# Attention's second 1024 tokens loaded in six transfers by token groups, and half of the state model's first input behind their transposes

## Chip, cores and metric

The kernel runs on one core of one Trainium2 chip. The metric is the device time of one execution in microseconds (us); less is better. A core has a matrix engine (TensorE, "PE" in the profile), a vector engine (VectorE, "DVE"), an activation engine (ScalarE, "ACT"), GpSimd ("POOL") and a queue engine (SyncE, "SP") that here does nothing but issue transfers. Sixteen DMA engines move the data. An engine executes its own instructions in order; between engines, semaphores make one wait for another.

## What is computed

Two independent models read two inputs of 2048 tokens x 448 features and give the two halves of one output of 2048 x 896. The first is an attention in which a token looks at eight tokens, at distances 0, 2, ..., 14 behind it, with 16 heads of 28. The second is a state-space model with 448 complex states.

```python
# first half: A (D = 448, H = 16, Dh = 28, W = 8, dil = 2)
qkv = x @ wqkv                                  # q, k, v
idx = pos[:, None] - arange(W) * dil            # masked where negative
logits = einsum("bhsd,bhswd->bhsw", q, k[idx]) * Dh ** -0.5
o = einsum("bhsw,bhswd->bhsd", softmax(logits), v[idx])
a = o @ wo
# second half: B
Lam_bar = exp(dt * Lam); B_bar = ((Lam_bar - 1) / Lam) * Bmat
h_t = Lam_bar * h_{t-1} + B_bar @ x_t           # complex, 2048 steps
y = 2 * real(C @ h) + x * Dskip
return concatenate([a, b], axis=-1)
```

## The kernel before

All work is cut into small operations, and a list written out by hand (`ORDER`, lines 32 to 61) gives the order in which they are put on the engines. A name of the list is an operation with its arguments; `@` gives the PSUM banks, and the last sign the engine that empties them.

**Attention.** Tokens are handled as two units of 1024, called u = 0 and u = 1. For both, the input has to stand transposed in the tile `xT` (features on the partitions). Its chunks are [128 features, 512 tokens]; chunk 3 holds the last 64 features of both 512-token halves. For u = 0, TensorE transposes the input. For u = 1 the DMA engines do: line 167 loads the tokens 1024 to 2047 into the second half of the buffer `xbuf` in three transfers, one for each range of columns, each for all four groups t of 128 rows (group t stands for the 128 tokens from 1024 + 128 t and the 128 tokens from 1536 + 128 t). Line 182 issues four DMA transposes, one for each t, from `xbuf` to `xT[:, 1]`. The operations `QK1..` (query and key projections, all four groups) and `V_4..`, `V_5..` (value projections; `V_4..` takes the groups 0 and 1, `V_5..` the groups 2 and 3) read the result. The first of them in `ORDER` are `V_411` and `V_410`; behind these comes `QK100`.

**The state model's input** is loaded by `x_load` (lines 174 to 177) into `xnB`, in four column blocks cb of 128 chunks: `x_load(0)` brings cb 0 and 1 in six transfers, `x_load(1)` cb 2 and 3. It is transposed by DMA later (`xt`, line 746, in the order cb 2, 0, 1, 3) into `xbuf`, when attention no longer needs that buffer. The weight `Bn` (line 187) is loaded between, and transposed by `BD` (line 722). The first operations that read all four transposed blocks are `BU200` and `BU100`, which begin the state model on TensorE.

**The queue engine.** Nearly all transfers are issued by SP, in program order: weights and attention's input; the three of line 167; the six of `x_load(0)`; the four transposes of line 182; four of `Bn`; the six of `x_load(1)`; four of `Cr` (the operation `LC`, lines 288 and 289); then `TD0` (line 451), the DMA transpose of the first unit's logits, which ScalarE writes in `lt` (line 442); then `xt` and `BD`. An issue that must wait holds back all that is behind it. The transfers take turns on eight semaphores, so an issue also waits until the transfer eight places before it has landed.

Of the kernel before, what the change touches and what calls it, by code (L numbers as in the profile page):

```python
# [14 lines left out]
S, D, H, DH, W = 2048, 448, 16, 28, 8  # L15
# [48 lines left out]
def kernel(  # L64
# [21 lines left out]
    SP = nc.sync  # L86
# [37 lines left out]
    xA_r = A_x[0].rearrange("(t p) d -> p t d", p=128)  # L124
# [38 lines left out]
        w_half(s, 0, D, 2 * D)  # L163

    xA1 = xbuf[:, 8 * D:].rearrange("p (t n) -> p t n", n=2 * D)
    for d0, d1, b, c in ((0, D, 8, 0), (D, 512, 12, 384), (512, 896, 12, 0)):
        SP.dma_start(xA1[:, :, d0:d1], xA_r[:, b:b + 4, c:c + d1 - d0])


    xnB = keep.tile([128, 4, T, D], BF16, tag="xnB")  # L170
    xP = xnB.rearrange("p c j d -> p c (j d)").rearrange("p c (a n) -> p c a n", a=2)
    xB_r = B_x[0].rearrange("(q p h a b) d -> h p q a b d", q=2, p=128, h=2, a=2)

    def x_load(hh):
        for d0, d1, b, c in ((0, D, 0, 0), (D, 512, 1, 384), (512, 896, 1, 0)):
            for q in range(2):
                SP.dma_start(xP[:, 2 * hh + q, :, d0:d1], xB_r[hh, :, q, :, b, c:c + d1 - d0])

    x_load(0)

    for t in range(4):
        SP.dma_start(xT[:, 1, :, 128 * t:128 * t + 128], xA1[:, t], transpose=True)

    Bn = s2.tile([128, G, 512], BF16, tag="Bn")
    for d0, d1, c in ((0, D, 0), (D, 512, 384)):
        for ri, b in enumerate((B_B_re, B_B_im)):
            SP.dma_start(Bn[64 * ri:64 * ri + 64, :, d0:d1], b[:, c:D].rearrange("(g p) d -> p g d", p=64))
    x_load(1)
    dsk = const.tile([128, 2 * D], BF16, tag="dsk")

    ident = const.tile([128, 128], BF16, tag="ident")
# [843 lines left out]
```

## Time and profile before

| | us |
|---|---|
| three runs | 125.88, 123.89, 125.00 |
| median | 125.0 |
| the profiled execution | 123.66 |
| its span, from the first to the last instruction | 121.9 |
| TensorE busy in the span | 117.4 |
| VectorE / ScalarE busy | 110.5 / 103.9 |
| granted TensorE clock | 1.00 of full speed |

The profile is of one execution. Its times count from the first instruction; 1.8 us of the 123.66 lie outside the span. "L258" is line 258 of the kernel; a line of a helper (258 is the matmul inside `part`, 114 the eviction) stands for many operations. `out<-in` names the tiles. "SPq" is an issue on SP's queue: its length is the time that SP needs to issue, not that of the transfer. "Time to landing" is from the start of an issue until the data is in place. A list of waits says which engine was held up by what. The chain of waits goes back from the last instruction, at each step to what released it.

### The profile page before, as it was taken

The numbers are of one execution on the slowest core, as the hardware profiler recorded it, in microseconds if no ns is written. First come the engines' busy times: TensorE is split into PE (matmuls) and PEld (weight loads), VectorE is DVE, ScalarE is ACT, GpSimd is POOL, SyncE is SP. The second block draws the span as 40 slices with busy tenths as digits, with TensorE's granted clock in tenths as the row PEclk, the third lists the DMA queues.
The fourth block names the chain that finished last, engine by engine and source line by source line (L and its number), as shares of the span: only waits on it lengthen the run. The fifth ranks groups of instructions, "written<-read, shape, count | busy, mean of one in ns | idle before, by whom it ended". The sixth has DMA issues, their size and how long they took to land.

```text
span 121.9 us, 2888 instructions
## 1 busy us (share of the span) xinstructions
PE 117.4 (96%) x1071; PEld 59.3 (49%) x1071; DVE 110.5 (91%) x198; ACT 103.9 (85%) x200; POOL 22.6 (19%) x49
## 2 busy tenths in 40 slices
PE   6989999999999999999999999999999999999990
PEld 6765434432434443363345544645665555555560
DVE  4378999999999999999999999999999999998561
ACT  0799999989999999999999999999999999980000
POOL 6823600000000000004999910000000000000000
PEclk9999999999999999999999999999999999999999
DMA  3999999999899999789869999999642504436642
GB/s 92 259 277 245 320 213 206 190 190 269 271 200 207 214 213 142 182 171 369 258 104 147 140 316 260 129 126 132 163 98 47 155 0 147 134 117 199 199 151 75
DMA packets 56661, 22.34 MB, mean 183 GB/s; under 512 B 42343, under 2 KB 56103, under 8 KB 56647
## 3 DMA queue, kind: packets, MB, share of 16 engines
q1 hardware_dynamic: 56440, 22.08, 83.6%
q8 instruction: 8, 0.13, 0.4%
q10 hardware_dynamic: 207, 0.07, 0.3%
q14 instruction: 6, 0.05, 0.1%
HBM read 9.86 MB, written 6.37 MB: 133 GB/s over the span
## 4 chain that ended last, share of the span: by engine, by line
PE 92%; DMA 4%; ACTq 1%; DVE 0%; issue 0%
PE ps L258 40%; PE ps L916 16%; PE ps L585 10%; PE ps L429 5%; PE ps L773 4%; PE ps L572 4%; DMA wzz<-in_A_wqkv_dram 4%; PE ps L373 3%; PE ps L846 1%; PE ps L941 1%; PE ps L374 1%; PE ps L433 1%; ACTq L150 1%; PE ps L499 1%; PE ps L385 1%; PE ps L785 1%
## 5 line engine op out<-in xcount | busy, mean ns | idle before, releaser
L417 DVE TENSOR_TENSOR pr<-qf,kf 128x2048 bf16<-128x2048 bf16 x24 | 27.7, 1219 | 0.2 <-ACT qf L114 0.2
L258 PE MATMUL ps<-xbuf,BT 128*128 128x512 bf16 (+1 forms) x112 | 24.1, 380 | 0.0
L916 PE MATMUL ps<-Cw,Z 128*128 128x448 bf16 x105 | 20.8, 352 | 0.0
L258 PE MATMUL ps<-xT,wq 128*128 128x512 bf16 (+1 forms) x72 | 15.8, 380 | 0.0
L916 PEld LDWEIGHTS <-Z 128*128 128x128 bf16 x105 | 10.3, 98 | 9.5
L258 PEld LDWEIGHTS <-BT 128*128 128x128 bf16 (+1 forms) x112 | 9.0, 97 | 11.7 <-issue 3.2
L585 PE MATMUL ps<-wo,oT 128*128 128x448 bf16 x64 | 13.4, 353 | 0.0
L258 PE MATMUL ps<-wq,xT 128*128 128x448 bf16 (+1 forms) x64 | 12.0, 353 | 0.0
L114 ACT CAST Z<-ps 128x512 bf16<-128x512 f32 (+1 forms) x23 | 11.4, 537 | 0.3 <-PE ps L258 0.2
L992 POOL MEMSET PT<- 128x4320 f32 x3 | 11.0, 3703 | 0.0
L258 PEld LDWEIGHTS <-wq 128*128 128x128 bf16 (+1 forms) x72 | 6.0, 97 | 8.7 <-issue 2.5
L734 ACT ACTIVATE ctmp<-Cw,c2t 64x448 f32<-64x448 bf16 x14 | 9.3, 666 | 0.2
L585 PEld LDWEIGHTS <-oT 128*128 128x128 bf16 x64 | 6.2, 98 | 5.7
L114 ACT CAST oT<-ps 128x512 bf16<-128x512 f32 x15 | 8.2, 626 | 0.0
L114 ACT CAST v_s<-ps 128x448 bf16<-128x448 f32 x16 | 8.2, 536 | 0.0
L258 PEld LDWEIGHTS <-xT 128*128 128x128 bf16 (+1 forms) x64 | 5.2, 97 | 6.3 <-issue 1.8
L968 POOL MEMSET Z<- 128x14 bf16 x1 | 0.1, 112 | 42.3 <-ACT ctmp L734 42.3
L114 ACT CAST qf<-ps 128x512 bf16<-128x512 f32 x12 | 7.0, 590 | 0.5 <-PE ps L258 0.5
L773 PE MATMUL ps<-Z,R 128*128 128x512 bf16 x21 | 7.3, 381 | 0.0
L114 ACT CAST kf<-ps 128x512 bf16<-128x512 f32 x12 | 7.0, 591 | 0.0
L114 ACT CAST ya<-ps 128x448 bf16<-128x448 f32 (+1 forms) x12 | 6.1, 552 | 0.2 <-PE ps L585 0.2
L926 DVE TENSOR_TENSOR xbuf<-ps,xnB 128x384 bf16<-128x384 f32 x8 | 4.4, 549 | 2.0 <-PE ps L916 2.0
(175 smaller groups left out, 228.2 us busy)
## 6 DMA issues: line engine op xcount, KB each, us to landing
PT<-pd SPq DMA_DIRECT2D x16, 156.0 KB, 4.3
out_dram<-ya SPq DMA_DIRECT2D x16, 112.0 KB, 1.7
out_dram<-xbuf SPq DMA_DIRECT2D x15, 112.0 KB, 1.8
pd<-Ak SPq DMA_DIRECT2D x2, 640.0 KB, 3.6
xbuf<-in_A_x_dram SPq DMA_DIRECT2D x2, 448.0 KB, 5.0
xnB<-in_B_x_dram SPq DMA_DIRECT2D x4, 224.0 KB
xnB<-in_B_x_dram SPq DMA_DIRECT2D x4, 192.0 KB, 4.2
pd<-oT SPq DMA_DIRECT2D x1, 640.0 KB, 5.1
```

The costliest lines, as they stand in the source:

```text
L114: (ACT.copy if e == "A" else V.tensor_copy)(o, i)
L258: PE.matmul(o, l, r, start=(first and i == 0), stop=(not first and i == len(pairs) - 1 and not more[s]))
L373: PE.matmul(p[:], wqk(m, slice(0, 128), kt), xT[:, 0, 4 * s + kt], start=(kt == 0), stop=False)
L417: V.tensor_tensor(t[:], q.unsqueeze(1).to_broadcast((128, 4, 512)), k4, ALU.mult)
L429: PE.matmul(acc[s][32 * i:32 * i + 32], E[:, f, ws, :], t[:, i, :], start=(f == 0 and ws == 0), stop=False)
L572: PE.matmul(p[32 * hh:32 * hh + 32, 128 * bl:128 * bl + n], v_s[:, t, 4 * hg + hh, :], PT[:, t % NS, (4 * hg + hh) // HS, (4 * hg + hh) % ...
L585: PE.matmul(p[:, 0:D], late["oT"][:, b // 4, hg, par, 128 * (b % 4):128 * (b % 4) + 128], late["wo"][:, hg, :], start=(hg == 0), stop=(hg ...
L734: ACT.activation(t[a:a + 64, 0:D], Cw[b:b + 64, g, :], ACTF.Copy, scale=c2t[a:a + 64, g:g + 1])
L773: PE.matmul(pp["z", g, j][:], rot(g, 0), late["Z"][:, g, j - 1, :], start=False, stop=True)
L916: PE.matmul(p[:, 0:D], z, Cw[:, g, :], start=(g == 0), stop=(g == G - 1))
L926: V.tensor_tensor(yo[:, 0:384], p[:, 0:384], xP[:, ct, j // 2, 512:896], ALU.add)
L992: POOL.memset(late["PT"][:, 4 * i:4 * i + 4].rearrange("p t g n -> p (t g n)").bitcast(F32), 0.0)
```

## The change

The load of attention's second unit is cut by token groups: three transfers for the groups 0 and 1, then three for 2 and 3, each half as large. `x_load` takes a list of blocks and brings one block after the other. The transfers of cb 1, three of the six of `x_load(0)`, are issued behind the four transposes. `x_load(1)` brings the same six transfers as before, with cb 2 whole before cb 3.

```diff
-    for d0, d1, b, c in ((0, D, 8, 0), (D, 512, 12, 384), (512, 896, 12, 0)):
-        SP.dma_start(xA1[:, :, d0:d1], xA_r[:, b:b + 4, c:c + d1 - d0])
+    for t in (0, 2):
+        for d0, d1, b, c in ((0, D, 8 + t, 0), (D, 512, 12 + t, 384), (512, 896, 12 + t, 0)):
+            SP.dma_start(xA1[:, t:t + 2, d0:d1], xA_r[:, b:b + 2, c:c + d1 - d0])
...
-    def x_load(hh):
-        for d0, d1, b, c in ((0, D, 0, 0), (D, 512, 1, 384), (512, 896, 1, 0)):
-            for q in range(2):
+    def x_load(hh, *qs):
+        for q in qs:
+            for d0, d1, b, c in ((0, D, 0, 0), (D, 512, 1, 384), (512, 896, 1, 0)):
                 SP.dma_start(xP[:, 2 * hh + q, :, d0:d1], xB_r[hh, :, q, :, b, c:c + d1 - d0])
 
-    x_load(0)
+    x_load(0, 0)
 
     for t in range(4):
         SP.dma_start(xT[:, 1, :, 128 * t:128 * t + 128], xA1[:, t], transpose=True)
+    x_load(0, 1)
...
-    x_load(1)
+    x_load(1, 0, 1)
```

## The prediction

> **What bounds the kernel now.** I read the page first, then the list of waits for TensorE, then the chain of waits in order of time.
>
> ```profile
> span 121.9 us, 2888 instructions
> PE 117.4 (96%) x1071; PEld 59.3 (49%) x1071; DVE 110.5 (91%) x198; ACT 103.9 (85%) x200; POOL 22.6 (19%) x49
> PE 92%; DMA 4%; ACTq 1%; DVE 0%; issue 0%
> ```
>
> TensorE is busy for 117.4 of 121.9 us, and 92% of the chain that ended last lies on it. The profiled execution took 123.66 us, so 1.8 us lie outside the span. The three runs took 123.89, 125.00 and 125.88: the profiled one is 1.34 below their median.
>
> ```profile
> PE ps L276 <- DVE wz L120: 1.1, 1, 1.1
> PE ps L386 <- DMA wzz<-in_A_wqkv_dram: 0.4, 1, 0.4
> ...
> 6.56 0.05 issue
> 6.61 0.28 PE ps L386
> ...
> 15.70 4.77 PE ps L258 x26
> 20.47 1.41 PE ps L429 x24
> 21.88 6.28 PE ps L258 x32
> ...
> 117.60 1.36 PE ps L941 x14
> 118.98 0.39 DVE xbuf L951
> ```
>
> The first two rows are all the waits that TensorE had, and both are over by 6.61 us, before the first changed instruction. From then on the chain is TensorE, piece against piece (15.70 + 4.77 = 20.47; 20.47 + 1.41 = 21.88), until the last matmul at 118.96. So in this execution the transposed second unit never held TensorE up. That is the first result: there is nothing here for an earlier arrival to win. A change of the loads can cost, where it makes TensorE wait, and can win only in executions that ran less smoothly than the profiled one.
>
> The timeline of TensorE has the two consumers that matter, and that of SP the issues around the change:
>
> ```profile
> 21.82 1.61 PE L258 MATMUL ps<-wq,xT 64*128 64x448 bf16 x8
> 23.26 2.75 PE L258 MATMUL ps<-xT,wq 128*128 128x512 bf16 x12
> ...
> 48.29 3.52 PE L258 MATMUL ps<-xbuf,BT 128*128 128x512 bf16 x18
> ```
>
> ```profile
> 9.09 1.69 SPq L167 DMA_DIRECT2D xbuf<-in_A_x_dram  x3
> 10.82 3.67 SPq L177 DMA_DIRECT2D xnB<-in_B_x_dram  x6
> 15.65 5.35 SPq L182 DMA_TRANSPOSE xT<-xbuf  x4
> 21.04 0.64 SPq L187 DMA_DIRECT2D Bn<-in_B_B_re_dram  x1
> ...
> 23.74 4.51 SPq L177 DMA_DIRECT2D xnB<-in_B_x_dram  x6
> ...
> 30.37 0.49 SPq L289 DMA_DIRECT2D Cr<-in_B_C_im_dram  x1
> 32.41 1.27 SPq L451 DMA_TRANSPOSE attn<-lt  x1
> 33.78 2.00 SPq L746 DMA_TRANSPOSE xbuf<-xnB  x1
> ...
> 38.03 6.31 SPq L746 DMA_TRANSPOSE xbuf<-xnB  x3
> ```
>
> By the order list, the eight matmuls from 21.82 are V_411 and V_410 (groups 0 and 1), those from 23.26 begin with QK100, which needs all four groups, and 48.29 is the first BU of the state model.
>
> **How thin the cover is.** The first and the last of the four transposes on SP's timeline, then the landing of one transpose of Cn in the list of transfers, then the landings of line 746:
>
> ```profile
> 15.65 1.34 SPq L182 DMA_TRANSPOSE xT<-xbuf  x1
> ...
> 19.70 1.30 SPq L182 DMA_TRANSPOSE xT<-xbuf  x1
> ```
>
> ```profile
> Cw<-Cn SPq DMA_TRANSPOSE x1, 2.7
> ```
>
> ```profile
> DMA to landing us min/median/max: 4.5/4.8/5.0
> ```
>
> The transpose of Cn, whose issue is about as long, needs 2.7 us from issue to landing; the larger ones of line 746 need 4.5 to 5.0. The last transpose of xT starts at 19.70. It cannot have landed before its issue ended (21.00), nor after 23.26, or QK100 had waited. With 2.7 it lands at 22.4, an estimate, 0.9 us before its use; the bounds of that margin are 0 and 2.26. The 4.5 is excluded by the missing wait. A margin of that kind is small beside the spread of the three runs (2.0 us), so in some of them QK100 may well have waited.
>
> **Part 1: six transfers for three.** The number of issues ahead of the transposes stays nine (3 + 6 before, 6 + 3 after), and I cost each like the x loads at the end of the stretch; SP's list of waits stands behind:
>
> ```profile
> 13.00 0.47 SPq L177 DMA_DIRECT2D xnB<-in_B_x_dram  x1
> 13.51 0.47 SPq L177 DMA_DIRECT2D xnB<-in_B_x_dram  x1
> ```
>
> ```profile
> SPq L182 <- DMA xbuf<-in_A_x_dram: 1.1, 1, 1.1
> SPq L177 <- DMA Bn<-in_B_B_im_dram: 0.7, 1, 0.7
> ```
>
> SP is through with the nine at 10.82 + 3.67 = 14.49 and then waits 1.1 us for the landing of line 167. After the change the first transpose needs only the first three pieces, half the bytes.
>
> ```profile
> xbuf<-in_A_x_dram SPq DMA_DIRECT2D x1, 448.0 KB, 5.0
> ```
>
> The first 448 KB of line 167 landed at 9.09 + 5.0 = 14.1. The three pieces of groups 0 and 1 are together 448 KB at the same place in the queue, so 14.1 is my value; the later bound is the third piece's issue at about 10.2 (9.09 + 2 x 0.56) plus the same 5.0, 15.2. So the first transpose starts at about 14.5 instead of 15.65, 1.15 us earlier; at worst 0.45. Groups 2 and 3 had landed at 15.65 before, and the third transpose's turn comes at 14.5 + 2 x 1.34 = 17.2, so it does not wait. The four issues end at 19.85 instead of 21.00, and the last transpose lands 1.15 us earlier (0.45 to 1.15; the DMA queue ahead of it is also shorter, which cannot help beyond its own issue). QK100's margin becomes about 2.0 us instead of 0.9. TensorE in the profiled execution: 0.0, since it did not wait.
>
> **Part 2: cb 1 behind the transposes.** Three issues of 0.51 each (13.00 to 13.51) are added to SP's way to Bn: 19.85 + 1.53 = 21.4 against 21.04, so Bn, x_load(1) and Cr are issued 0.35 us later; at the worst bound 1.05. The wait of 0.7 above, an x load that waits for the Bn transfer eight issues before it, moves along and stays about as long. SP is through with Cr at 30.86; the next issue, TD0, starts at 32.41 because of ScalarE:
>
> ```profile
> 31.32 1.06 ACT L442 ACTIVATE lt<-ps 128x512 bf16<-128x512 f32 x2
> ```
>
> The logits are ready at 32.38. So 1.55 us of waiting lie in SP's queue there, and the 0.35 to 1.05 vanish in it. Without that cover the line 746 transposes would each come 0.35 to 1.05 later, towards the BU at 48.29. The data of cb 1 itself is read by the second of the three transposes from 38.03, at about 40.1; issued around 21 with 4.4 to 4.6 us to landing (rows below), it has over 13 us to spare. x_load(1) only changes the order of its six issues, with cb 2, which is needed first, whole earlier: nothing. No other engine's queue is passed.
>
> The DMA engines are the other thing that is shifted. The busy times by stretch have their mean share and GB/s in the last two columns:
>
> ```profile
> 15.00:17.00 2.00, 2.00 (x12) 0.76 (x11) 1.80 (x3) 2.00 (x5) 0.00 (x0) 1.00 1.15 279
> ...
> 21.00:24.00 3.00, 3.00 (x32) 1.30 (x21) 3.00 (x4) 3.00 (x7) 0.00 (x0) 1.00 0.91 184
> ...
> 33.00:34.00 1.00, 1.00 (x6) 0.48 (x5) 1.00 (x2) 0.96 (x3) 0.00 (x0) 1.00 0.52 132
> 34.00:48.00 14.00, 14.00 (x126) 5.85 (x123) 13.79 (x17) 13.91 (x25) 0.00 (x0) 1.00 1.15 197
> ```
>
> The 448 KB of cb 1 take 1.6 us at 279 GB/s. They move from before the transposes to behind; the transposes finish 1.15 earlier; so Bn and what follows come about 0.45 us later on the engines. Between 33 and 34 the engines are only half busy, which absorbs 0.48. Behind it, the last line 746 transpose is issued at about 42.2 (38.03 + 6.31 less one issue of 2.1) and lands at most 5.0 later, 47.2, against the BU at 48.29: another 1.1 us of cover. Cost on TensorE: 0.0.
>
> **A rule against the change.** The small pieces of 64 columns become 32 KB. In the list of transfers the neighbours in the same stretch are:
>
> ```profile
> xnB<-in_B_x_dram SPq DMA_DIRECT2D x2, 192.0 KB, 4.4
> xnB<-in_B_x_dram SPq DMA_DIRECT2D x2, 32.0 KB, 4.6
> ```
>
> A transfer of 32 KB lands as late after its issue as one of 192 KB, while issues go out every 0.51 us: what a transfer waits for is the queue ahead of it, and a fixed part, if there is one, runs beside the others. The Trainium skill's page "DMA: Bandwidth & Descriptors", in "Rules for kernel authors", says to join small transfers, since under 64 KB one pays mostly overhead, and its section on the anatomy of one DMA fits a fixed part of about 2.0 us for the GpSimd path. If that part were paid one after the other, three added transfers would cost 6 us by that page; the two rows above speak against it.
>
> **Sum.** 123.66 + 0.0 + 0.0 = 123.66 for an execution like the profiled one. What the other runs have above it (0.23, 1.34, 2.22) the trace cannot place. If it is QK100 that waits in them, up to 1.15 us of each goes, leaving 123.66, 123.85 and 124.73, median 123.85. If it lies elsewhere (the start up to 6.61 us hangs on first loads, which the change does not touch), the median stays at 125.0. I take the middle, 124.4.
>
> **The rivals.**
>
> First, the surplus goes wholly: 123.85. For it speaks the thin margin of 0.9 us; against it, that the start hangs on transfers just as much. Chance 0.27.
>
> Second, slower: the added transfers cost the queue of the DMA engines a time of their own. The cheapest landing among all transfers of the buffer xbuf bounds it:
>
> ```profile
> DMA to landing us min/median/max: 1.5/2.6/5.0
> ```
>
> Three times 1.5 are 4.5 us. 0.48 go into the idle stretch at 33, 1.1 into the margin ahead of BU at 48.29; 2.9 remain as a wait of TensorE there: 126.6 for the profiled execution, 127.9 with the surplus of the median. It decides from 1.6 us of delay on (0.48 + 1.1). For it: the engines are at a share of 1.15 from 34 to 48 and catch up nothing there. Against it: the two rows above, and that the number of rows and their lengths, and so the bytes, stay as they are. Chance 0.13.
>
> Third, the change does not do what it says: the first transpose still waits for all six pieces, the last issued at about 11.9 (9.09 + 5 x 0.56) and landing 4.4 to 5.0 later, at 16.9 at the latest. Then the transposes come 1.25 us later, and QK100 loses its 0.9 and waits 0.35. SP reaches Bn at 16.9 + 5.35 + 1.53 = 23.8, 2.75 late, of which 1.2 is left at TD0, about what the 1.1 ahead of BU and the later BU take up: 124.0, with the surplus 125.4. Against it: the pieces of the groups 2 and 3 lie in other rows of the buffer than what the first transpose reads. Chance 0.08.
>
> Fourth, faster by more than the bound: TensorE would have to be rid of 1.2 us below the profiled execution, in which it does not wait after 6.61. Only a comparison against unlucky runs of before gives that, with 122.4. Chance 0.07.
>
> **The numbers.** The forecast, no wait changed on TensorE and half of the surplus gone, has 0.45 and its own range of 123.4 to 125.9. A difference below about 2% (2.5 us) cannot be told from none, as the three runs lie 1.6% apart. Forecast, first and third rival lie within it: 0.45 + 0.27 + 0.08 = 0.80. Slower 0.13, faster 0.07. The range from 123.4 to 126.4 holds these three with the spread of the runs and leaves out the other 0.20.
>
> **What would show it.** In the profile after: the first transpose of xT at about 14.5 and no wait for xbuf in SP's list; Bn's first issue at 21.4; TD0 still directly behind the logits of ScalarE; QK100 and the first BU at 23.3 and 48.3, and no new row in TensorE's list of waits. A first transpose at 15.6 or later would show the third rival; a wait ahead of the first BU, with landings of line 746 above 5.0, the second. The forecast would be wrong if TensorE waited in the middle of the span.

## The result, and the profile after

The kernel after takes 125.62 us (median of 16 runs, 124.97 upwards), the kernel before 124.91 beside it (16 runs, 123.60 to 125.88). The ratio is 1.0101, with a 95% interval of 1.0063 to 1.0138: slower by about 1%. (A ratio, here and below, is of the means of the fast runs: runs over 1.5% above the fastest of the same kernel, three of before and one of after here, are left out.) That is less than the 2% that a few runs can tell from no change, but more than the spread of these sixteen leaves open. The forecast was 124.4, 0.6 us below the 125.0 that I knew then; the time went the other way. It lies inside the range of 123.4 to 126.4.

The profiled execution after took 125.89 us, 2.23 more than the profiled one before, at the same granted clock of 1.00. From its page, the busy times and the shares of the chain that ended last:

```profile
span 124.2 us, 2892 instructions
PE 118.0 (95%) x1071; PEld 59.8 (48%) x1071; DVE 110.9 (89%) x198; ACT 103.8 (84%) x200; POOL 22.6 (18%) x49
PE 81%; DMA 8%; SPq 6%; issue 0%; DVE 0%
```

The engines do the same work as before, but only 81% of the chain lies on TensorE now, against 92%: 6% are issues on SP's queue and 8% transfers. The list of what TensorE waited for has two new rows of the middle of the span:

```profile
PE ps L260 <- DMA xbuf<-xnB: 1.4, 1, 1.4
...
PE ps L260 <- ACT v_s L114: 0.2, 1, 0.2
```

The chain in order of time (start, length, what) shows which transfer that is:

```profile
30.69 6.13 PE ps L260 x30
36.82 0.96 SPq L748
...
37.84 1.96 SPq L724
...
39.84 2.05 SPq L748
...
41.94 2.09 SPq L748
...
44.07 5.97 DMA xbuf<-xnB
...
50.17 3.51 PE ps L260 x18
```

It leaves TensorE at 36.8, runs over SP issues end to end, then over the last transpose from its issue at 44.07 to its landing at 44.07 + 5.97 = 50.04, and comes back to TensorE at the first `BU`, 50.17. That the first of these issues waited for TensorE at 36.82 is not so: in the profile before, the same issue was through at 35.78, although TensorE's times up to there are the same to 0.02 us. What is late is to be looked for further back on SP's queue. (Line 748 is the old 746, 260 the old 258.) Before, that `BU` started at 48.29. Of the 1.88 us between, 1.40 are this wait; the other 0.48 are small slips ahead of it, the wait of 0.2 for ScalarE among them. The remaining 0.35 of the 2.23 lie behind TensorE's work on the state model's output, which starts its last group 1.82 late, and I have not followed them.

SP's timeline says why the transposes came late:

```profile
9.37 4.02 SPq L168 DMA_DIRECT2D xbuf<-in_A_x_dram  x6
13.43 1.49 SPq L178 DMA_DIRECT2D xnB<-in_B_x_dram  x3
15.04 5.37 SPq L183 DMA_TRANSPOSE xT<-xbuf  x4
20.45 1.62 SPq L178 DMA_DIRECT2D xnB<-in_B_x_dram  x3
22.12 0.66 SPq L189 DMA_DIRECT2D Bn<-in_B_B_re_dram  x1
...
24.84 5.45 SPq L178 DMA_DIRECT2D xnB<-in_B_x_dram  x6
30.33 0.47 SPq L290 DMA_DIRECT2D Cr<-in_B_C_re_dram  x1
...
31.55 1.54 SPq L290 DMA_DIRECT2D Cr<-in_B_C_im_dram  x1
33.13 0.50 SPq L291 DMA_DIRECT2D Cr<-in_B_C_im_dram  x1
33.73 1.28 SPq L453 DMA_TRANSPOSE attn<-lt  x1
35.10 2.68 SPq L748 DMA_TRANSPOSE xbuf<-xnB  x1
...
39.84 6.40 SPq L748 DMA_TRANSPOSE xbuf<-xnB  x3
```

Of the same view of before, the prediction showed all that stands against this but the first `Cr` issue:

```profile
28.37 0.40 SPq L288 DMA_DIRECT2D Cr<-in_B_C_re_dram  x1
```

SP reaches `Bn` 1.08 us later (22.12 against 21.04; 0.28 of that it had already at line 168, 9.37 against 9.09, ahead of all that was changed), and is through with `Cr` 2.77 later (33.63 against 30.86). Before, SP waited there for ScalarE's logits until 32.41; those 1.55 us are eaten up. `TD0` goes out 1.32 later, now held by nothing but SP itself, and the last three line 748 transposes begin 1.81 later (39.84 against 38.03).

**The last transfer is also longer.** The time from issue to landing of the state model's transposes had a median of 4.8 us before. After, the list of transfers, which has landings for some of them only, says

```profile
DMA to landing us min/median/max: 4.8/4.8/4.8
```

but the last one, by the chain, took 5.97. The busy times by stretch (TensorE, its weight loads, VectorE, ScalarE, GpSimd, granted clock, DMA share, GB/s) and the queue of instructions among the DMA queues in the first of these half microseconds (packets, MB, share):

```profile
46.50:47.00 0.50, 0.50 (x16) 0.28 (x12) 0.50 (x2) 0.50 (x1) 0.00 (x0) 1.00 1.25 239
47.00:47.50 0.50, 0.50 (x16) 0.13 (x8) 0.50 (x1) 0.50 (x2) 0.00 (x0) 1.00 4.52 85
47.50:48.00 0.50, 0.50 (x12) 0.12 (x4) 0.50 (x2) 0.50 (x3) 0.00 (x0) 1.00 0.01 1
48.00:48.50 0.50, 0.50 (x20) 0.14 (x16) 0.50 (x1) 0.50 (x2) 0.00 (x0) 1.00 0.09 9
```

```profile
q8 instruction: 1, 0.02, 15.5%
```

From 47.0 to 48.5 next to nothing moves (85, 1 and 9 GB/s), and directly ahead of it one block of instructions is fetched. With the usual 4.8 us the last transpose would have landed at 48.87, close to the 48.77 at which TensorE was ready (50.17 less 1.40). So by this working about 1.2 of the 1.4 us come from this stop, under which SP's lateness had moved the transpose. In the profile before, a fetch falls in the same half microsecond, 46.5 to 47.0,

```profile
q8 instruction: 1, 0.02, 11.7%
```

but the last transpose, issued at 42.2, had landed by 47.2 at the latest, going by the longest landing of the list, 5.0.

Two suspicions came out of this, which the runs below were to tell apart. The first: SP's own issue time is the cause, and bytes and the place of the data do not matter. The second: the stop sets the price. The rivals were that one of the two parts alone costs it (the split, or the move), that the added transfers cost the DMA engines a time of their own, and that the bytes behind the transposes crowd the later loads.

### The profile page after: what moved, and what is told of

Read it like the earlier page. It is cut to its first block, busy times and chain, and to the rows that moved or that the text cites. A ratio compares the mean times of both kernels' runs of the same rounds, so it can differ in the third digit from the quotient of the medians.

```text
span 124.2 us, 2892 instructions
## 1 busy us (share of the span) xinstructions
PE 118.0 (95%) x1071; PEld 59.8 (48%) x1071; DVE 110.9 (89%) x198; ACT 103.8 (84%) x200; POOL 22.6 (18%) x49
## 4 chain that ended last, share of the span: by engine, by line
PE 81%; DMA 8%; SPq 6%; issue 0%; DVE 0%
PE ps L260 33%; PE ps L918 16%; PE ps L587 10%; DMA xbuf<-xnB 5%; SPq L748 4%; PE ps L775 4%; DMA wq<-in_A_wqkv_dram 4%; PE ps L574 4%; PE ps L375 3%; PE ps L431 2%; SPq L724 2%; PE ps L848 1%; PE ps L387 1%; PE ps L943 1%; PE ps L376 1%; PE ps L501 1%
## 5 line engine op out<-in xcount | busy, mean ns | idle before, releaser
L114 DVE CAST Z<-ps 128x256 bf16<-128x256 f32 (+1 forms) x12 | 5.8, 506 | 0.7 <-PE ps L260 0.4
```

The costliest lines, as they stand in the source:

```text
L114: (ACT.copy if e == "A" else V.tensor_copy)(o, i)
```

## The experiments

Each was timed beside the kernel before on the same chip; a ratio is to that, with its 95% interval.

**The two parts one at a time.** First only the split, with both column blocks of the state model's input ahead of the transposes:

```diff
-    x_load(0, 0)
+    x_load(0, 0, 1)
...
-    x_load(0, 1)
```

> Attention's second 1024 tokens come in six transfers, but both blocks of the state model's first input stay ahead of the transposes. Theory M (the loads that were moved behind the transposes are what costs: they leave the DMA engines underfed and are paid back behind Bn): as the kernel before, ratio 0.995 to 1.004, no wait of TensorE ahead of the first BU; SP reaches Bn at 21.5 to 22.0 and the wait ahead of TD0 takes that up. Theory S (the three added issues and transfers are what costs): as the changed kernel, ratio 1.007 to 1.013, a wait of 1 to 2 us ahead of the first BU.

Then only the move, with line 167's three transfers as before:

```diff
-    x_load(0)
+    x_load(0, 0)
...
+    x_load(0, 1)
```

> Three transfers as before the change, but half of the first input is loaded behind the transposes. Theory M: the first transpose starts at 15.6 as before, Bn is reached at 22.6, and the first BU waits 1.5 to 3 us: ratio 1.010 to 1.022. Theory S: without the three added issues there is no loss, ratio 0.995 to 1.004.

The split alone: 125.36 us, 1.0108 (1.0052 to 1.0164). The move alone: 126.46, 1.0177 (1.0117 to 1.0236). SP's timeline of the split, then of the move:

```profile
17.39 5.36 SPq L183 DMA_TRANSPOSE xT<-xbuf  x4
22.80 0.64 SPq L188 DMA_DIRECT2D Bn<-in_B_B_re_dram  x1
...
33.69 1.27 SPq L452 DMA_TRANSPOSE attn<-lt  x1
```

```profile
10.92 2.37 SPq L177 DMA_DIRECT2D xnB<-in_B_x_dram  x3
16.03 5.35 SPq L182 DMA_TRANSPOSE xT<-xbuf  x4
...
23.10 0.67 SPq L188 DMA_DIRECT2D Bn<-in_B_B_re_dram  x1
...
34.12 1.28 SPq L452 DMA_TRANSPOSE attn<-lt  x1
```

Each part alone costs as much as both or more, so neither is innocent, and they do not add up. Both lengthen SP's way to `Bn`. The split puts twelve issues ahead of the transposes instead of nine. The move adds none, but with the three issues gone from ahead of the transposes SP is through at 13.29 and then stands idle until 16.03, for the landing of line 167; the three issues that filled this wait before now come behind it. Both reach `Bn` later than 21.04 and `TD0` later than 32.41. In the move that is SP's doing: it is through with `Cr` at 34.00, and the logits had been ready at 32.76. In the split it is not: SP is through at 33.19 and waits for the logits, which are themselves late:

```profile
32.60 1.06 ACT L443 ACTIVATE lt<-ps 128x512 bf16<-128x512 f32 x2
```

TensorE was already 0.62 us behind at 21.02 (20.40 before), from the first loads, and then `QK100` waited 0.2 us for `xT`, whose transposes had begun at 17.39 instead of 15.65. So the split loses a part of its time ahead of `TD0`, in another way than the kernel after.

In both the first `BU` waits, 1.3 and 1.2 us. Both lists of waits put that on ScalarE's `lt`, here the logits of the second unit. It cannot be that: in the profile before, `BU` started at 48.29, ahead of them,

```profile
48.42 1.09 ACT L442 ACTIVATE lt<-ps 128x512 bf16<-128x512 f32 x2
```

and in the move it started at 50.40, while the second of them ran until 50.69. What ScalarE did ahead of `lt` was done by 49.70 there. That leaves a transfer, which the list does not name.

**Fewer bytes behind.** The kernel after, with 64 of the 448 columns of the `Cr` loads:

```diff
-            SP.dma_start(Cr[:, 0:3, i], c[0:384].rearrange("(t p) n -> p t n", p=128))
+            SP.dma_start(Cr[:, 0:3, i, 0:64], c[0:384, 0:64].rearrange("(t p) n -> p t n", p=128))
...
+        POOL.memset(Cr[:, :, :, 64:D], 0.0)
```

> The changed kernel, with only 64 of the 448 columns of the four Cr loads (the rest of Cr is set to zero, so C of the state model is incomplete): the same issues on SP, 0.67 MB less for the DMA engines ahead of TD0. If the lateness is that of the DMA engines' queue (the issues of Cr and of the first line 748 transpose are held back by a full queue), the last line 748 transpose lands 1.5 us or more earlier and the wait ahead of the first BU (1.4 us) is gone: ratio 0.99 to 1.002. If it is SP's own time, TD0 still starts at 33 or later and the ratio stays at 1.007 to 1.013.

124.77, 1.0052 (1.0016 to 1.0089), `TD0` at 32.86, a wait of 0.6 us at the first `BU`. About half of the loss is gone. SP came earlier by 0.87 us at `TD0`, but 0.65 of it was there at the first `Cr` issue (29.68 against 30.33), ahead of all that this run leaves out, and one of the `Cr` issues still took 1.40 us. So this run does not show whether bytes bear on SP's time, and it does not separate the two suspicions.

**The kernel before once more**, for a profile of one of its longer runs:

> The kernel before once more, for its profile: its 16 times lie in two groups, six at 123.6 to 123.9 and ten at 124.7 to 125.9. If this execution falls in the upper group, the list of TensorE's waits names the wait that separates the groups: QK100 behind the transposes of line 182 (prediction), or the first BU behind those of line 746, or the first loads. In the lower group the profile is as the one shown, without a wait after 6.6 us.

It took 124.84, and so belongs with the upper of the two groups into which the 16 runs of before fall (six from 123.60 to 123.94, ten from 124.66 on). From TensorE's timeline:

```profile
23.48 0.81 PE L258 MATMUL ps<-xT,wq 128*128 128x512 bf16 x3
...
49.53 1.67 PE L258 MATMUL ps<-xbuf,BT 128*128 128x512 bf16 x7 [0.96 <-ACT lt L442]
```

The matmul at 23.48 is `QK100`, with no wait in brackets. The wait that makes this run longer than the profiled one is at the first `BU`, 0.96 us: the same place as in the kernel after. Again it cannot be `lt`, and again little moves on the DMA engines ahead of it:

```profile
48.50:49.00 0.50, 0.07 (x8) 0.00 (x0) 0.47 (x2) 0.50 (x2) 0.00 (x0) 1.00 0.92 74
49.00:49.50 0.50, 0.00 (x0) 0.00 (x1) 0.46 (x2) 0.50 (x2) 0.00 (x0) 1.00 0.20 32
```

`TD0` was on time in this execution (32.63, the logits at 32.60), so a stop can cost this `BU` its time without SP being late there.

**The fetch of instructions.** If the stop belongs to the fetch, it must move when another number of TensorE's instructions stands ahead. The warm-up matmuls, which compute nothing, were changed for that. With 32 instructions fewer (in the kernel before, then in the kernel after):

```diff
-        for _ in range(22):
-            PE.matmul(p[:, 0:128], wz[:], wz[:], start=True, stop=True)
+        for _ in range(6):
+            PE.matmul(p[:], wz[:], wz[:].unsqueeze(1).to_broadcast((128, 4, 128)), start=True, stop=True)
```

> The kernel before, with the 22 warm-up matmuls of 128 columns written as 6 of 512: 32 instructions of TensorE fewer ahead of all others, about the same time. Theory F (the stop of the DMA transposes around 47 us belongs to the fetch of TensorE's next 16 KB of instructions, which comes at a fixed place of its program): the fetch that stood at 46.5 to 47.3 comes about 1 us later, and the stop falls behind the landing of the last line 746 transpose. No wait ahead of the first BU, the upper group of times is gone: ratio 0.991 to 0.997. Theory L (the stop belongs to the load of Dskip, issued behind the last transpose, or to another thing): two groups as before, ratio 0.998 to 1.003.

> The same in the changed kernel. Theory F: the last line 748 transpose is no longer stopped or only at its end; the wait ahead of the first BU falls from 1.4 us to 0.7 or less, what is left is the lateness of SP and of the queue alone: ratio to before 0.998 to 1.006. Theory L: wait and ratio as for the changed kernel, 1.007 to 1.013.

And with 52 more:

```diff
-        for _ in range(22):
+        for _ in range(14):
             PE.matmul(p[:, 0:128], wz[:], wz[:], start=True, stop=True)
+        for _ in range(34):
+            PE.matmul(p[0:32, 0:32], wz[:, 0:32], wz[:, 0:32], start=True, stop=True)
```

> The kernel before, with the warm-up written as 14 matmuls of 128 columns and 34 of 32 columns: 52 instructions of TensorE more. Theory F: the fetch comes at 43 to 44.5 and the stop falls into one of the last two line 746 transposes in every execution: the first BU waits 0.3 to 1.5 us, no times of the lower group, ratio 1.001 to 1.010. Theory L: two groups as before, ratio 0.998 to 1.003.

Fewer: 124.13, 0.9982 (0.9948 to 1.0016) in the kernel before, which decides nothing, as the interval reaches into both ranges expected; 125.14, 1.0037 (1.0004 to 1.0070) in the kernel after, whose profile has no wait at the first `BU` any more. There the fetch lies between 47.0 and 47.5, and little moves from 48.5 on (88 and 0 GB/s in the first two half microseconds). But the stop is not all that differs. SP reached `Bn` at 22.12, as in the kernel after, and yet was through with `Cr` at 31.86, so that `TD0` went out right behind the logits of 32.73:

```profile
32.75 1.43 SPq L453 DMA_TRANSPOSE attn<-lt  x1
```

So in this execution the cover of the prediction did hold, and the run does not show what moving the stop is worth by itself. More: 123.94, 0.9968 (0.9929 to 1.0008) in the kernel before. Its stretches, and the DMA queues of the first of them:

```profile
42.50:43.00 0.50, 0.50 (x4) 0.29 (x3) 0.50 (x2) 0.50 (x2) 0.00 (x0) 1.00 2.31 194
43.00:43.50 0.50, 0.50 (x5) 0.23 (x3) 0.50 (x1) 0.50 (x2) 0.00 (x0) 1.00 2.52 7
43.50:44.00 0.50, 0.50 (x4) 0.26 (x3) 0.50 (x2) 0.50 (x1) 0.00 (x0) 1.00 0.08 8
```

```profile
q8 instruction: 1, 0.02, 11.0%
```

The fetch came 4 us earlier, and the stop with it. The loss that I expected from an earlier stop did not come: there the first `BU` is not held up, because more time is left behind the stop to catch up in (285 to 291 GB/s from 44.5 to 47.0, where the profile before has 139 to 217). But a stop of the same look comes at 49.0 to 50.0, 43 and 7 GB/s, and no packet of instructions falls between 43.0 and 50.0. In the kernel after, the same edit had no such effect:

> The changed kernel with the warm-up of the 52 more instructions alone (the Dskip load where it was, since behind the third Cn transpose it made ScalarE wait 1.2 to 1.7 us). The fetch and its stop come near 43, ahead of the last line 748 transpose, and can be caught up in part, as in the kernel before with the same warm-up (its last transpose landed at 47.7). If the loss of the change is later issue plus the stop on the last transpose: that transpose lands at 48.5 to 49.3, the first BU waits 0 to 0.8 us, ratio to before 0.999 to 1.005. If the later issue alone makes the loss: 49.5 or later, ratio 1.007 to 1.013.

126.16, 1.0100 (1.0052 to 1.0149). The profile (an execution of 125.33) has no wait at the first `BU`, but one of 0.2 us later, at the transfer `PT<-pd`. It is not SP's lateness at `TD0`: SP was through with `Cr` at 32.53, and `TD0` went out at 32.87, right behind the logits of 32.84. Against the profile before, TensorE is 0.47 us late at the first `BU` and 1.23 at the last group of attention's products with `PT` (90.09 against 88.86), so 0.76 are lost between. With 32 fewer the kernel after loses 0.80 in the same stretch (0.35, then 1.15); the kernel before with a changed warm-up loses nothing there (0.29, then 0.28 and 0.27). This is a second place of loss. What makes it is not known, and the run did not come out as expected. The kernel before with 52 more was run again, to see whether it is a better kernel:

> The kernel before with the 52 more warm-up instructions, whose ratio of 0.9968 (0.9929 to 1.0008) leaves open whether it beats before: if the stop ahead of the first BU is what makes the upper group of times, 0.993 to 0.999 with an upper bound below 1; if that was chance, 0.999 to 1.003.

124.76, 1.0004 (0.9961 to 1.0048): it is not.

**Another suspect for the stop**, the load of `Dskip` that SP issues behind the transposes. In the kernel before, its operation `LD` was moved in the order list:

```diff
-... ci2. LD CD2 E_12 ...
+... ci2. CD2 E_12 ...
-... V_010@17 CD0 P151 ...
+... V_010@17 CD0 LD P151 ...
```

> The kernel before, with the load of Dskip (LD) behind the third transpose of Cn instead of ahead of the first. Theory F: the stop stays at 47 to 48 and the two groups of times stay, ratio 0.998 to 1.004. Theory L: no stop at 47 to 48, the upper group is gone, ratio 0.991 to 0.997.

124.79, 1.0011 (0.9978 to 1.0044), and the first `BU` still waits 1.0 us behind a stop (2 and 10 GB/s from 48.0 to 49.0), with no load of `Dskip` under way yet: it is not the load. Two kernels had this edit and the 52 instructions more together, on the kernel before and on the kernel after:

> The kernel before with both things that stop the transposes around 47 us moved: the fetch by 52 more instructions of TensorE in the warm-up (it comes near 43) and the Dskip load behind the third transpose of Cn. If these two stops are what separates its two groups of times, all times lie at 123.7 to 124.4: ratio 0.992 to 0.998, no wait ahead of the first BU. If there is another cause, the groups stay: 0.998 to 1.002.

> The changed kernel with the same two things moved. If its loss is the later issue of the line 748 transposes together with the stop, half or more of it goes: the last transpose lands at 48 to 49 instead of 50, ratio to before 0.997 to 1.004. If the later issue alone costs it, the ratio stays at 1.007 to 1.012.

125.16, 1.0072 (1.0040 to 1.0103), and 126.26, 1.0176 (1.0134 to 1.0218). Both tell little, because the edit made a wait of its own: `Dskip` now came so late that ScalarE waited for it, 1.2 us in the first of them and 1.7 in the second, where the first `BU` waits another 0.8.

**SP's time by itself.** First the kernel after without the two small `Cr` loads (and so with two issues fewer on SP's way to `TD0`):

```diff
             SP.dma_start(Cr[:, 0:3, i], c[0:384].rearrange("(t p) n -> p t n", p=128))
-            SP.dma_start(Cr[0:64, 3, i], c[384:448])
...
+        POOL.memset(Cr[0:64, 3], 0.0)
```

> The changed kernel without the two small Cr loads (rows 384 to 447 of C are set to zero, so 64 columns of the state model's output are incomplete): two issues less on SP ahead of TD0, 0.11 MB less for the DMA engines (0.4 us at 290 GB/s). If the lateness at TD0 is SP's own time, TD0 starts at 32.4 to 32.8 instead of 33.7, the line 748 transposes follow 1 us earlier, and the ratio to before is 0.998 to 1.005. If it is the queue of the DMA engines, TD0 starts at 33.2 or later and the ratio stays at 1.006 to 1.012.

124.94, 1.0052 (1.0020 to 1.0084). `TD0` is back at 32.60, but the transposes still fall under the stop, and the first `BU` waits 0.9 us. So both were removed together, the two issues and, by the 52 warm-up instructions, the stop:

> The changed kernel without the two small Cr loads (rows 384 to 447 of C set to zero) and with the warm-up of 52 more instructions: SP's lateness at TD0 and the stop on the last line 748 transpose taken away together. If these two make the loss of the change: ratio to before 0.995 to 1.003, no wait ahead of the first BU. If a third cause is there (the warm-up with 52 more instructions left 1.010 by itself, without a wait ahead of BU): 1.005 to 1.012.

124.36, 1.0009 (0.9969 to 1.0048). The first `BU` no longer waits; it starts at 48.66. But neither did it in the kernel after with the 52 more alone, and there too `TD0` was on time. So the traces do not show what the two issues fewer bring beyond that. The one profiled execution, of 125.09, is no help: it loses 0.98 us behind the first `BU`, half of it waiting for `PT`.

Last, the reverse: the kernel before, with three loads of 1 KB into a tile that nobody reads, behind the four transposes. Their 3 KB are less than a hundredth of the 448 KB of cb 1:

```diff
+    few = const.tile([128, 3, 4], BF16, tag="few")
+    for i in range(3):
+        SP.dma_start(few[:, i], A_wqkv[0:128, 4 * i:4 * i + 4])
```

> The kernel before with three more SP issues behind the four transposes, each a load of 1 KB that nothing reads: SP's time alone, no loads moved and no bytes to speak of. If SP's time is the cost (TD0 later than the logits, the line 746 transposes behind it): SP reaches Bn at 22.6, TD0 starts at 33 or later, ratio 1.004 to 1.012. If it is the DMA engines' work that was moved: TD0 within 0.4 us of before (32.4 to 32.8), ratio 0.998 to 1.003.

126.05, 1.0127 (1.0063 to 1.0191). SP's timeline, then TensorE's:

```profile
21.49 1.54 SPq L186 DMA_DIRECT2D few<-in_A_wqkv_dram  x3
23.07 0.66 SPq L191 DMA_DIRECT2D Bn<-in_B_B_re_dram  x1
...
33.52 1.28 SPq L455 DMA_TRANSPOSE attn<-lt  x1
...
39.77 6.42 SPq L750 DMA_TRANSPOSE xbuf<-xnB  x3
```

```profile
50.33 1.02 PE L262 MATMUL ps<-xbuf,BT 128*128 128x512 bf16 x4 [1.18 <-DMA xbuf<-xnB]
```

With the loads of attention and of the state model left in their order, three issues on SP's queue bring the whole loss, at the same places: `Bn` late, `TD0` at 33.52 (the logits were ready at 32.70), the last transposes from 39.77, and a wait of 1.18 us at the first `BU`. So three issues more, with no load of use moved, are enough.

It is not SP's time alone, though. Between `Bn` and `TD0` SP has two waits that the kernel before has not:

```profile
SPq L292 <- DMA xnB<-in_B_x_dram: 0.6, 1, 0.6
SPq L293 <- DMA xnB<-in_B_x_dram: 0.5, 1, 0.5
```

Without these 1.1 us `Cr` would have been through by 32.3, ahead of the logits. They are waits for loads of `x_load(1)`, and from 23.0 to 24.5, behind the three tiny loads, the DMA engines moved 2, 3 and 0 GB/s, while `Bn` was issued only from 23.07 on. That the late issues left the engines without work is the likely reading; that the tiny rows held up the queue is not excluded. And as in the kernel after, the last transpose landed late, 6.19 us after its issue at 44.01; with 4.8 it would have been there at 48.81, before TensorE was ready at 49.15. So here too late issue and stop make the wait together.

## Why the prediction was wrong

**Nothing to win: right.** The transposes of `xT` started earlier, at 15.04 instead of 15.65, and neither `V_411` (21.84 against 21.82) nor `QK100` (23.28 against 23.26) came earlier for it. The forecast of 14.5 for the first transpose was too early by half a microsecond, inside its bound of 15.2: nothing waited for the data any more, but the nine issues themselves ended at 14.92 instead of 14.49, 0.28 of it because SP came to them later, the rest because they took 5.55 us instead of 5.40. The margin of `QK100` was thinner than the 0.9 I gave it: where the profile after lists the landing of these transposes, it took 3.0 to 3.5 us, not the 2.7 of `Cn`, which puts the margin before at 0.1 to 0.6 by estimate. In the split alone, whose transposes came 1.74 later, `QK100` did wait.

**The step that failed: part 2, "the 0.35 to 1.05 vanish in it", with "Cost on TensorE: 0.0".** The cover was sized right: 1.55 us, up to `TD0`. What was to go into it was counted only as far as `Bn`. There it was 1.08 us late, at my worst bound. But from `Bn` to the end of `Cr` there are fourteen issues, and I let them take as long as before, 9.82 us. They did not: the six of `x_load(1)` took 5.45 us instead of 4.51, the four of `Cr` 3.30 (30.33 to 33.63) instead of 2.49 (28.37 to 30.86). A part of it is a wait that I had said "moves along and stays about as long":

```profile
SPq L178 <- DMA Bn<-in_B_B_im_dram: 1.0, 1, 1.0
```

It is 0.3 longer than the 0.7 of before. The rest is in the issues' own length: one of `Cr` took 1.54 us, its neighbours 0.47 to 0.66. Not all of that is the change's doing. The second profile of the kernel before also has a `Cr` issue of 1.58 us and took 10.51 for the fourteen; the kernel after took 11.51, and with 32 instructions fewer 9.74, where the same 1.08 at `Bn` did vanish in the cover. One execution's length was no constant to add to. In the profile after, together 2.77 us against a cover of 1.55, and the 1.22 that are left reappear as the 1.32 of `TD0`. The prediction named what an uncovered delay would do, "the line 746 transposes would each come 0.35 to 1.05 later, towards the BU at 48.29"; it was 1.8, and the 1.1 us of margin there did not hold it.

**The landing: sized without its tail.** "Lands at most 5.0 later" came from the landings of one execution. Beside the stop it was 5.97, and a longer execution of the kernel before already lost 0.96 us at the same `BU`, with `TD0` on time. So this term failed as well: a cost of 0.0 needed both the cover and the landing to hold.

**The surplus: wrong place.** I guessed that the longer runs of before wait at `QK100` and took half of their surplus off, which made the forecast 0.6 us faster. The one such run that was profiled does not wait at `QK100` but at the first `BU`, which the change makes worse. The rival "the surplus goes wholly" falls with it.

**The rivals.** The first transpose did not wait for all six pieces. The slower rival had the place right, the wait ahead of the first `BU`, but not the mechanism: it let the DMA engines pay for every added transfer, and the sign that I gave for it, a landing above 5.0 us, appeared for another reason, the stop. The time from issue to landing, where it is listed, has the same median of 4.8 us before, after and with the three tiny loads. What remains of the rival is that with the three tiny loads a part of SP's lateness is a wait for loads to land. The rule that the Trainium skill's page "DMA: Bandwidth & Descriptors" gives under "Rules for kernel authors", to join small transfers, pointed the right way; what these runs show is 0.51 us of SP's time for an issue (1.54 for three); of the fixed 2.0 us, which the prediction took from that page for the GpSimd path, they show nothing.

**What stays open**: why the transposes stop, and whether the fetch does it; why one issue takes 0.5 us and its neighbour 1.5; how much of the 1% belongs to the late issues and how much to the stop, since no run takes one away and leaves the other as it was; and what the kernel after loses behind the first `BU` in executions that do not wait there. With 52 more instructions it is still 1% slower, and without the two issues as well it is at 1.0009.

## What to carry to other kernels

An engine that only issues transfers is a chain like any other: each issue here costs half a microsecond to two, and a change that looks free for the DMA engines must be followed along that queue, every issue and wait, up to the first transfer that a busy engine needs. A wait in such a queue is a cover only for the lateness that arrives at it, not for the one that is known at the first step; three 1 KB loads that were of no use to anyone overran 1.55 us of it, with the waits behind them, and cost 1.3%. And the length of such a stretch, read from one profile, is not a constant: the same fourteen issues took 9.4 to 11.5 us here. When runs of one kernel fall into two groups, profile one of each before placing the difference: it may lie exactly where the change presses.

## What the runs showed of the hardware

I had not expected that data would stop moving behind a fetch of instructions. TensorE's program comes in blocks; the page after has

```profile
q8 instruction: 8, 0.13, 0.5%
```

eight packets of 16 KB. In the kernel after one of them (46.5 to 47.0 us) was followed by a stop of 1.5 us in which the DMA transposes moved 1 to 85 GB/s, and with 52 instructions more ahead of it, in the kernel before, fetch and stop both came about 4 us earlier. With the three tiny loads the fetch lies between 47.5 and 48.0, and the next three half microseconds move 74, 13 and 7 GB/s. That the fetch causes the stop is inferred from their moving together, and it is not the whole of it: the fetch at 31.5 to 32.0 in the kernel after, with plain loads under way, was followed by 282 and 342 GB/s, and with the 52 more the stop at 49.0 to 50.0 has no fetch ahead of it. The Trainium skill's page "Runtime: NRT & Kernel Launch", section "Instruction fetch mechanics", gives blocks of 16 KiB fetched over a DMA queue of the sequencer's own, which agrees with this row, and calls the cost mostly hidden. For TensorE's instructions that holds here, as no wait for them stands in its list of waits; for the transposes under way, if the inference is right, it does not, by the 5.97 us instead of 4.8.
